# Issuing y's transfers in the block that computes y, and one product of four units a block later

## The chip, the core and the metric

The kernel runs on one core of one Trainium2 chip. The metric is device time in microseconds of one execution. The engines are TensorE (PE, with its weight loads PEld), VectorE (DVE), ScalarE (ACT), GpSimd (POOL) and SyncE (SP), whose queue issues nearly all DMA transfers. Each engine works through its own instructions in the order in which the program writes them, and waits at semaphores for the others. Lines are given as L1167, line 1167 of the kernel before.

## What is computed

The first part is a linear recurrence over 768 steps for 4 batches of 8 heads, with a 40 by 40 state each; the second is a feed-forward with a hardswish on the 3072 tokens of 320 features that come out of it.

```python
for t in range(S):
    y[:, :, t] = np.einsum('bhd,bhde->bhe', rt, state)
    Sa = np.einsum('bhde,bhe->bhd', state, at)
    state_decay = state * wt[:, :, None, :] - np.einsum('bhd,bhe->bhde', Sa, bt)
    state = state_decay + np.einsum('bhd,bhe->bhde', vt, kt)
...
h = x @ w_in
relu6 = np.clip(h + 3.0, 0.0, 6.0)
g = h * relu6 / 6.0
return (g @ w_out).astype(np.float32)
```

## The kernel before

**Units.** The recurrence is cut into 24 units, numbered 0 to 23: 64 steps of two batches with all heads. Four units form a group (`NU = 4`). Within a unit the steps are turned into matrix products: a first set, `prepare`, needs only the inputs and may run ahead (W and its running products `gam`, A, B, K, F, E, `factor`, EV); a second, `step`, needs the state left by the unit before (RT, VT, R, C, S, U, UT, rS, H, and `ysn`, which gives y and the new state). EV (L745) is scores times v: 32 small matmuls whose result `R` adds to much later. A triangular inverse of each group (`invert`, L779) runs on DVE in small steps between the other work.

**y to the feed-forward.** `ysn` (L1055) multiplies on PE (L1064), DVE adds (L1071), and POOL scales by `gam` into the tile `yg` (L1072). Then `move` issues four transfers from `yg` into `xt`, the layout that the feed-forward reads (L1111), and `move2` another four (L1116) and sets `ready[i]`. All eight are on SP's queue, between the fetches of inputs (`fetch`, L451; L478 for R and A, L490 for W, B and K, L487 for V) and the outputs (L1239). A fetch is written behind the instruction that has read the old contents of its tile, and waits for it.

**Order in blocks.** From unit 4 on, the program writes four blocks per unit, numbered here from 0 (`a_block`, L1505). Unit i's `ysn` stands in block 4(i-4)+4, its transfers in the next one. A unit's `prepare` begins at block `begins[i]`: units 8 to 11 at blocks 0, 3, 6 and 9, from 12 on every four blocks. Units 8 to 11 follow `CLOSE_STAGES`, the others `AHEAD_STAGES`; both lists give the stages for successive blocks. A block has two parts: the own unit's stages and the `prepare` of units that began at a multiple of four are in the first, the others in the second. `together` (L1468) writes a part: first the PE work of its stages in the order of `PRODUCTS`, then what DVE, ACT, POOL and SP do with the results in the order of `RESULTS`. Products of a part share pairs of PSUM banks, 512 columns each; two pairs take turns, and the next user of a pair waits until what was in it is read.

**The feed-forward between.** Behind each part, `feed` writes a few pieces of the feed-forward (`feed_forward`, L1140). Its jobs are half units (i, r), in a fixed list. A job has four expand pieces (L1167, x by `win`, into two PSUM tiles `h`), a short piece for the last 64 features (L1167 with 64 rows, or L1180 in a doubled 64-column form when no VT, B or factor stands beside it), ACT's and DVE's hardswish `gt` (L1189, L1190), and four contract pieces (L1215). The contract pieces of a job are written behind the expand pieces of the next one. If the next job's unit is not in `ready`, the contract pieces come at once and then nothing, until the unit is ready. The number of pieces per block is fixed by rates: 2.8 for units 4 to 6, then 3.5 or 4.5 times 8/9, and 6.2 where an inversion runs. A piece is 8 PE records (each float32 matmul leaves two), about 1 us.

After the last block the rest of the feed-forward is written without anything between.

Of the kernel before, what the change touches and what calls it, by code (L numbers as in the profile page):

```python
# [31 lines left out]
def kernel(  # L32
# [43 lines left out]
    B, H, T, D = r.shape  # L76
# [485 lines left out]
    def begun_beside():  # L562

        begin = -(-(SCAN + 1) // 16) * 16
        for n, name in enumerate("KB"):
            x = area[:, begin + n * H * JOIN:begin + (n + 1) * H * JOIN]
            nc.gpsimd.memset(x, 0.0)
            beside[name] = x.rearrange("p (h t) -> p h t", h=H)
        beside["E"] = grp.tile([P, H, BL], F32, name="E", tag="U", bufs=1)
        nc.gpsimd.memset(beside["E"][:], 0.0)  # L570
        for name in "rgam", "RT":
            beside[name] = tmp.tile([P, NPR, P], F32, name=name, tag="rgam", bufs=2)
# [191 lines left out]
    def in_turn(stages, order):  # L764

        for name in order:
            yield from stages[name]()
            shared[0] = None
            yield DONE
# [510 lines left out]
    third, F, group_F = [], None, []  # L1280
# [11 lines left out]
    def prepared(i):  # L1292
        nonlocal F
        if i >= NK:
            return None
        if i % NU == 0:
            F = lazy_F()
        return prepare(i, F)
# [145 lines left out]
    for _ in range(18):  # L1444
# [5 lines left out]


    EARLY_STAGES = [["fade"], ["RT", "VT"]]
    OWN_STAGES = EARLY_STAGES + [[], ["R", "C", "S"], ["U", "UT", "rS"], ["H"], ["ysn"],
                                 ["move", "move2"]]
    AHEAD_STAGES = [["W", "gam"], ["A", "B"], ["F", "K"], ["E", "factor"], ["EV"]]
    CLOSE_STAGES = [["W", "gam"], ["A", "B"], ["F", "K", "factor"], ["E"], ["EV"]]


    PRODUCTS = ["W", "S", "K", "VT", "B", "factor",
                "ysn", "EV", "R", "C", "U", "UT", "rS", "H", "E", "F"]  # L1460
    RESULTS = ["ysn", "W", "VT", "EV", "R", "S", "C", "A", "B", "move", "move2",
               "U", "UT", "rS", "F", "K", "fade", "H", "E", "factor", "RT", "gam"]
    TURNS = PRODUCTS[:3]
    WIDTH = {"R": NPR * D, "U": 512, "UT": 0, "ysn": NPR * JOIN, "EV": NPR * D}
# [3 lines left out]
    def together(stages):  # L1468
# [3 lines left out]
        def finish():  # L1472
            begun.sort(key=lambda x: RESULTS.index(x[0]))
            for _, rest in begun:
                for _ in rest:
                    pass
            begun.clear()
            shared[0] = open_half[0] = None
            ring.clear()
            ring.extend(TURNS_IN)  # L1480
# [24 lines left out]
    def a_block(m):  # L1505

        if coming and begins[coming[0]] == m:
            u = coming.popleft()
            close = coming and begins[coming[0]] < m + BLOCKS
            ahead[u, m] = prepared(u), CLOSE_STAGES if close else AHEAD_STAGES  # L1510
        i, early = (m + len(EARLY_STAGES)) // BLOCKS + NU, m + len(EARLY_STAGES)
        if m >= 0 and early % BLOCKS == 0 and i < NK:
            own[i, m] = step(i), OWN_STAGES
        parts = {}, {}
# [21 lines left out]
    begun_beside()  # L1536
    own[NU, -len(EARLY_STAGES)] = step(NU), OWN_STAGES
    for _ in in_turn(own[NU, -len(EARLY_STAGES)][0], [x for stages in EARLY_STAGES for x in stages]):
# [62 lines left out]
```

## Time and profile before

| | us |
|---|---|
| median of 3 runs (lowest to highest) | 781.25 (779.56 to 782.09) |
| profiled execution | 778.37 |
| its span, first to last instruction | 776.6 |
| PE busy | 714.2 |
| DVE busy | 508.0 |
| ACT busy | 310.1 |
| POOL busy | 176.4 |
| PE expand, L1167 | 228.9 |
| PE contract, L1215 | 230.4 |

The profiled execution is one execution of the program, recorded by the profiler; all positions below are microseconds from its first instruction. In a line of the timeline the first number is the start and the second the duration; in brackets is how long the engine stood idle before it and what ended the wait. The granted clock is the share of full speed at which the chip lets TensorE run; its mean over this execution is 0.964.

### The profile page before, as it was taken

To read this page: it belongs to the slowest core of one execution; us is meant where nothing else is said; L and a number is where in the kernel's file an instruction comes from. 1 tells how busy PE (TensorE), PEld (TensorE's weight loads), DVE (VectorE), ACT (ScalarE), POOL (GpSimd) and SP (SyncE) were. 2 spreads that over 40 slices of the span, in tenths; PEclk is the share of its full clock that TensorE was granted. 3 is DMA by queue.
4 is the path that set the end of the run, shared out by engine and by line. 5 is a ranking of instruction groups with operands and counts; after the bars stand their busy time and mean duration, and the time that the engine had idled before them with its cause. 6 is when DMAs were issued, how large, how long until landed. Compare 5 with 4: busy or idle time off the path is not lost.

```text
span 776.6 us, 33024 instructions
## 1 busy us (share of the span) xinstructions
PE 714.2 (92%) x14568; PEld 604.4 (78%) x14568; DVE 508.0 (65%) x1007; ACT 310.1 (40%) x644; POOL 176.4 (23%) x323
## 2 busy tenths in 40 slices
PE   5735888999899989999999999999999999999997
PEld 4634787878778778788888788888788888888885
DVE  7899967588657799456798356898446982323210
ACT  2377865323444334443334443234443224412211
POOL 7403110322233303123213122304122201110000
PEclk9956789999999999999999999999999999999999
DMA  9685553420434412233313223313232100110000
GB/s 124 122 189 133 113 169 60 78 40 19 78 62 85 74 43 53 43 66 67 59 43 57 55 62 67 59 44 61 52 62 53 29 19 24 35 35 12 13 18 19
DMA packets 176000, 48.44 MB, mean 62 GB/s; under 512 B 159216, under 2 KB 174576, under 8 KB 175856
## 3 DMA queue, kind: packets, MB, share of 16 engines
q1 hardware_dynamic: 171552, 45.58, 29.5%
q8 instruction: 115, 1.88, 1.0%
q10 hardware_dynamic: 4304, 0.74, 0.7%
q14 instruction: 29, 0.24, 0.1%
HBM read 37.62 MB, written 3.93 MB: 54 GB/s over the span
## 4 chain that ended last, share of the span: by engine, by line
PE 71%; DVE 13%; SPq 5%; issue 4%; ACT 3%; DMA 3%; POOL 0%; DVEq 0%; ACTq 0%; POOLq 0%
PE h L1167 24%; PE o L1215 22%; PE pair L554 4%; PE pair L1064 4%; DVE prod L804 2%; PE h L1180 2%; DVE x L810 2%; SPq L490 2%; PE one L506 2%; DVE prods L603 2%; PE pair L927 1%; PE pair L1007 1%; PE pair L516 1%; PE pair L968 1%; PE pair L1023 1%
## 5 line engine op out<-in xcount | busy, mean ns | idle before, releaser
L1167 PE MATMUL h<-xt,win 128*128 128x128 f32 (+1 forms) x2000 | 228.9, 282 | 8.4 <-DMA xt<-yg 4.2
L1167 PEld LDWEIGHTS h<-xt,win 128*128 128x128 f32 (+1 forms) x2000 | 211.9, 192 | 24.2 <-issue 7.7
L1215 PE MATMUL o<-wout,gt 128*128 128x320 f32 x768 | 230.4, 443 | 0.0
L1215 PEld LDWEIGHTS o<-wout,gt 128*128 128x128 f32 x768 | 138.7, 191 | 50.6 <-issue 0.6
L1189 ACT ACTIVATE gt<-h,three 128x512 f32<-128x512 f32 x96 | 62.5, 685 | 108.3 <-PE h L1167 86.0
L1190 DVE SCALAR_TENSOR_TENSOR gt<-gt,h 128x512 f32<-128x512 f32 x96 | 61.8, 680 | 63.8 <-ACT gt L1189 63.7
L578 DVE COPY_PREDICATED area<-mask,pair 128x512 f32<-128x512 int32 x56 | 40.7, 726 | 61.2 <-PE pair L554 42.7
L804 DVE TENSOR_TENSOR prod<-x 128x30 f32<-128x30 f32 (+9 forms) x180 | 63.8, 354 | 8.9 <-POOL x L789 2.5
L810 DVE TENSOR_TENSOR x<-x,prod 128x30 f32<-128x30 f32 (+9 forms) x180 | 63.3, 352 | 5.4
L1072 POOL TENSOR_TENSOR yg<-ys,gam 128x512 f32<-128x512 f32 x20 | 25.5, 1274 | 129.1 <-DVE ys L1071 87.5
L725 POOL TENSOR_TENSOR KBt<-K,rgt 128x320 f32<-128x320 f32 x22 | 19.0, 865 | 141.1 <-ACT rgt L714 118.7
L603 DVE TENSOR_TENSOR_SCAN prods<-area,start 128x528 f32<-128x528 f32 x24 | 40.9, 1708 | 3.8 <-ACT area L599 3.7
L1071 DVE TENSOR_TENSOR ys<-pair,ys 128x512 f32<-128x512 f32 x20 | 13.8, 690 | 41.3 <-PE pair L1064 41.3
L757 ACT ACTIVATE EV<-pair 64x320 f32<-64x320 f32 x44 | 19.0, 431 | 37.9 <-PE pair L752 37.5
L1064 PE MATMUL pair<-area,KBt 64*64 64x104 f32 x1280 | 32.4, 250 | 0.0
L1233 ACT ACTIVATE ob<-o 128x320 f32<-128x320 f32 x22 | 9.6, 435 | 56.7 <-PE o L1215 35.2
L614 DVE TENSOR_TENSOR_SCAN area<-area,start 128x528 f32<-128x528 f32 x24 | 31.2, 1301 | 0.8
L1064 PEld LDWEIGHTS pair<-area,KBt 64*64 64x64 f32 x1280 | 29.9, 133 | 1.5 <-issue 1.4
L872 ACT ACTIVATE tinv<-pair 32x256 f32<-32x256 f32 x48 | 18.0, 374 | 32.6 <-PE pair L862 32.1
L993 POOL COPY area<-V 128x320 f32<-128x320 f32 x20 | 9.0, 452 | 82.4 <-DVE area L645 51.3
L938 ACT ACTIVATE VT<-pair 128x512 f32<-128x512 f32 x22 | 13.1, 597 | 30.2 <-PE pair L705 16.2
L931 DVE TENSOR_TENSOR RR<-pair,EV 128x320 f32<-128x320 f32 x22 | 10.7, 486 | 20.8 <-PE pair L554 14.8
(289 smaller groups left out, 1093.4 us busy)
## 6 DMA issues: line engine op xcount, KB each, us to landing
V<-in_v_dram SPq DMA_DIRECT2D x96, 40.0 KB
out_dram<-ob SPq DMA_DIRECT2D x47, 80.0 KB
R<-in_r_dram SPq DMA_DIRECT2D x92, 40.0 KB
B<-in_b_dram SPq DMA_DIRECT2D x42, 80.0 KB
K<-in_k_dram SPq DMA_DIRECT2D x42, 80.0 KB
W<-in_w_dram SPq DMA_DIRECT2D x37, 80.0 KB
A<-in_a_dram SPq DMA_DIRECT2D x37, 80.0 KB
xt<-yg SPq DMA_DIRECT2D x72, 40.0 KB
```

The costliest lines, as they stand in the source:

```text
L554: nc.tensor.matmul(out=o[i][half(q), n ^ (2 * q * placed), :], lhsT=lhs[half(i, D), n ^ (2 * q * swap), half(q)], rhs=rhs[half(i, D), n, h ...
L578: nc.vector.copy_predicated(out=x[:].rearrange("p (i h) t -> p i h t", i=2), mask=mask8, data=o[2])
L603: nc.vector.tensor_tensor_scan(out=prods[:].rearrange("p r m i -> p (r m i)"), data0=wm[:, 0:SCAN], data1=start[:], initial=0.0, op0=ALU.m ...
L614: nc.vector.tensor_tensor_scan(out=back, data0=back, data1=start[:], initial=0.0, op0=ALU.mult, op1=ALU.add)
L804: nc.vector.tensor_tensor(out=pv, in0=_ap(x[:], (i + 1) * L + i, [[L, n], [0, i]]), in1=_ap(x[:], i * L, [[0, n], [1, i]]), op=ALU.mult,)
L810: nc.vector.tensor_tensor(out=rest, in0=rest, in1=pv, op=ALU.add)
L1064: nc.tensor.matmul(out=both[q][half(s), pr, :], lhsT=o[name][half(q), h * D:h * D + SLOT], rhs=beside[name][half(q), 4 * rs + 2 * (s ^ (q ...
L1072: nc.gpsimd.tensor_tensor(out=yg[:], in0=m["ys"][:].rearrange("p r q t -> p r (q t)"), in1=o["G"][:], op=ALU.mult)
L1167: nc.tensor.matmul(out=hp[c][:, i, :], lhsT=lhsT, rhs=rhs, start=(begun[c] == 0), stop=(begun[c] == 3 * NQ - 1))
L1189: nc.scalar.activation(out=gt[:], in_=hp[c][:], func=AF.Relu, bias=three[:], scale=1.0)
L1190: nc.vector.scalar_tensor_tensor(out=gt[:], in0=gt[:], scalar=6.0, in1=hp[c][:], op0=ALU.min, op1=ALU.mult)
L1215: nc.tensor.matmul(out=op[:], lhsT=gts[c][:, n, :], rhs=wout[:, c * HJ + r * NQ + n, :], start=((split or r == 0) and c == 0 and n == 0), ...
```

## The change

Three lists are edited. `ysn`, `move` and `move2` stand in one block, so that each unit's transfers are written in the block of its `ysn`. In `RESULTS` the two come directly behind `ysn` and `W`, ahead of all else in that part. In `CLOSE_STAGES` an empty block is put ahead of EV: for units 8 to 11 it goes from blocks 4, 7, 10 and 13 to 5, 8, 11 and 14.

```diff
-    OWN_STAGES = EARLY_STAGES + [[], ["R", "C", "S"], ["U", "UT", "rS"], ["H"], ["ysn"],
-                                 ["move", "move2"]]
+    OWN_STAGES = EARLY_STAGES + [[], ["R", "C", "S"], ["U", "UT", "rS"], ["H"],
+                                 ["ysn", "move", "move2"]]
     AHEAD_STAGES = [["W", "gam"], ["A", "B"], ["F", "K"], ["E", "factor"], ["EV"]]
-    CLOSE_STAGES = [["W", "gam"], ["A", "B"], ["F", "K", "factor"], ["E"], ["EV"]]
+    CLOSE_STAGES = [["W", "gam"], ["A", "B"], ["F", "K", "factor"], ["E"], [], ["EV"]]
...
-    RESULTS = ["ysn", "W", "VT", "EV", "R", "S", "C", "A", "B", "move", "move2",
+    RESULTS = ["ysn", "W", "move", "move2", "VT", "EV", "R", "S", "C", "A", "B",
                "U", "UT", "rS", "F", "K", "fade", "H", "E", "factor", "RT", "gam"]
```

`ready[i]` is set in `move2`, so it too is set a block earlier. No instruction is added or taken away.

## The prediction

> **What bounds the kernel now.** I read the page's busy shares first, then the waits of the TensorE queue (PE) from 200 us on, then the timelines around them. PE carries the span:
>
> ```profile
> PE 714.2 (92%) x14568; PEld 604.4 (78%) x14568; DVE 508.0 (65%) x1007; ACT 310.1 (40%) x644; POOL 176.4 (23%) x323
> ```
>
> Most of PE's idle time lies in the first 110 us, ahead of what the change touches. From 200 us on, PE's waits by engine and line are (total us, times, longest):
>
> ```profile
> PE h L1167 <- DMA xt<-yg: 4.2, 3, 1.8
> PE pair L752 <- DVE area L645: 1.9, 1, 1.9
> PE h L1167 <- DVE gt L1190: 1.4, 3, 0.7
> PE pair L1023 <- ACT UT L1013: 1.1, 1, 1.1
> PE pair L554 <- DVE E L578: 0.6, 1, 0.6
> ```
>
> So the rest of the kernel is PE's work plus about 9 us of waits, and PE executes in the order written. The change adds no instruction; it can only remove waits, make new ones, or reorder. I therefore count waits, against the profiled execution: 778.37 us, span 776.6. That run is 2.88 us under the median of 781.25 us; the result is put on the median.
>
> **What it removes.** First the three waits for y's transfers, 4.2 us. One of them:
>
> ```profile
> 316.04 3.12 SPq L1111 DMA_DIRECT2D xt<-yg  x4
> 320.45 3.55 PE L1167 MATMUL h<-xt,win 128*128 128x128 f32 x31 [1.66 <-DMA xt<-yg]
> ```
>
> Unit 7's y is ready at 306.67 (POOL's product at 305.40, 1.27 us), but its transfers stand behind A's in SP's queue and start at 316.04; matmuls start 1.29 us after the fourth issue ends (319.16). Issued in y's own block, behind W alone (307.23, 1.35 us), they start about 308.6 and are down 10 us before PE needs them. Units 11 and 15 are alike. **Gain 4.2.**
>
> Second, unit 11's EV (L752). The columns are start, duration, operation; then the granted clock in two stretches:
>
> ```profile
> 279.58 0.68 PE L752 MATMUL pair<-V,E 64*64 64x40 f32 x32 [1.91 <-DVE area L645]
> 280.18 2.02 PE L1167 MATMUL h<-xt,win 128*128 128x128 f32 x8
> 282.00 3.16 PE L1215 MATMUL o<-wout,gt 128*128 128x320 f32 x8
> ```
> ```profile
> 276.87:280.28 3.41, 1.50 (x41) 1.00 0.00 0
> 280.28:283.69 3.41, 3.41 (x12) 0.50 0.42 91
> ```
>
> PE stood 1.91 us behind DVE, which runs the inversion there. A block later DVE has passed that point: **gain 1.9**. The stretch after it ran at half clock: eight records took 1.82 us to the next start where 1.00 is usual (243.87 to 244.87), and the next eight 2.99 where 2.26 is usual (287.55 to 289.81). **Gain 1.6.** (The Trainium skill, "TensorE: Matmul & The Clock Gate", Part 1, has the clock halve after at least one idle window of about 3.4 us. Here 1.91 us of idle in one such window was enough, and 1.66 us ahead of 320.45 was not. By the page this 1.6 would not exist and the sum below would be +6.2; the row decides, so the page's result gets no chance of its own.)
>
> Third, waits for gt, 0.69, 0.33 and 0.34 us (270.89, 390.69, 503.73). They come where a job's last expand piece falls behind ysn; with pieces a little ahead it falls in front. I take the last two, **gain 0.7**; at the first, DVE is full and the next wait for it (E, 0.60 us at 274.99) takes it over. Fourth, the short piece: counting the order through all blocks, 25 instead of 19 are in the doubled 64-column form, 0.92 us (301.98 to 302.90) against 1.00 (272.38 to 273.38): **gain 0.5**. Sum of gains: 8.9.
>
> **What it adds.** The one place where the feed-forward's order changes is unit 4. In block 4 three pieces are issued behind ysn: two contract pieces of job (3,0), then a third. Now unit 4 is not yet ready, so the third is a contract piece of (3,1) and the stream runs dry until block 6. After the change `ready[4]` is set ahead of them, so the third is unit 4's first expand piece, and PE meets it before the data:
>
> ```profile
> 214.36 0.62 PE L752 MATMUL pair<-V,E 64*64 64x40 f32 x32
> 214.91 2.42 PE L1215 MATMUL o<-wout,gt 128*128 128x320 f32 x8
> 216.79 1.28 POOL L1072 TENSOR_TENSOR yg<-ys,gam 128x512 f32<-128x512 f32 x1 [0.89 <-DVE ys L1071]
> 218.34 1.34 PE L1215 MATMUL o<-wout,gt 128*128 128x320 f32 x4
> 219.59 3.14 SPq L1111 DMA_DIRECT2D xt<-yg  x4
> ```
>
> y is there at 216.79+1.28 = 218.07; four issues take 3.14, the landing 1.29: 222.50. PE arrives at 218.34 less 0.55 (unit 8's EV, gone from this block): 217.79. **Loss 4.7**, and as a whole window is idle, half clock behind it, **loss 1.6** by the row above. Nothing hides it: PE had no wait over 0.5 us between 205 and 270, and everything behind it in order shifts.
>
> Next, PSUM. Products of a part share pairs of banks, 512 columns each, and two pairs take turns. In block 8 factor and F of unit 10 (256+256) fill one pair. With EV of unit 9 in the same part it is factor+EV, and F takes the other; so unit 6's R in block 9 must wait for factor's copy, which ACT does behind F's six. In the trace F's multiply starts at 239.74 and the copy (L714) ends at 243.02, 3.28 later; where PE waits for such a copy it starts 0.38 after it (U at 226.91, copy's end 226.53). PE needs 0.6+1.0+0.5 = 2.1 from F to R, so the wait is 3.7-2.1 = 1.6, I take **loss 1.5** (bounds 0.5 and 1.8).
>
> Last, SP's queue, which from 229 to 266 us never rests, as units 9 to 11 come three blocks apart:
>
> ```profile
> 235.39 4.68 SPq L478 DMA_DIRECT2D R<-in_r_dram  x8
> 240.18 2.65 SPq L478 DMA_DIRECT2D A<-in_a_dram  x4
> 242.87 2.58 SPq L487 DMA_DIRECT2D V<-in_v_dram  x4
> 245.56 1.95 SPq L490 DMA_DIRECT2D B<-in_b_dram  x2
> 247.64 1.27 SPq L490 DMA_DIRECT2D K<-in_k_dram  x2
> 248.96 3.67 SPq L1111 DMA_DIRECT2D xt<-yg  x4
> ```
>
> Unit 5's eight transfers (248.96 to 255.13, 6.2 us) move ahead of V, B and K. B of unit 11 is landed at 249.42 by the packets' record, 1.9 after its last issue; PE uses it at 251.03: cover 1.6. I count both from unit 10's W on PE (228.62). R's fetch starts when RT is turned, 6.8 after it; with gt of job (4,0) now ahead on ACT and DVE, 7.5. From there to B's last issue 12.1 now, plus 6.2, plus 1.2 for unit 3's output, which falls in here: 19.5; landing 1.9: 28.9. PE comes 22.4 after W now; five contract pieces (1.2 each) for four expand and a short one (5.1 together) add 0.9, R's wait 1.5: 24.8. **Loss 4.1** (bounds 0 and 5), and half clock again, **loss 1.6** (or 0). The moves ahead of A in later blocks cost nothing: SP stands 43.8 us in 13 places ahead of A's fetch for DVE's turn of A (L528) as it is, and A is next used three or more blocks on.
>
> Losses 4.7+1.6+1.5+4.1+1.6 = 13.5; gains 8.9; net +4.6 us: 783.0 against the profiled execution's 778.4, **785.8 us** against the median, 0.6% slower.
>
> **Rivals.** (A) SP keeps up and B is in time. For it: the estimate subtracts two long chains. Against it: 6.2 us are put ahead of a cover of 1.6. Then 5.7 falls away: -1.1, 780.1. (B) Faster: PE's 4.7 us at unit 4 let ACT and SP catch up, so neither R nor B is late. It decides from the point where SP starts R under 2 us after W of unit 10 instead of 7.5. Then 7.2 falls away: -2.6, 778.6. Against it: R's fetch starts from DVE's transposes, which shift with PE. (C) DVE is busy without rest from 263 to 316 us, so PE, once EV no longer waits, meets DVE at the next product (F at 316.75 has 2.4 us of cover): the 3.5 is given back, +8.1, 789.4. Against it: one or two more pieces lie in front by then, 1 to 2 us. (D) The order at unit 4 stays as it is, so only the waits for y and EV go (-7.7) and R and B come (+7.2): 780.7. The job list speaks against it.
>
> **Numbers.** Forecast 0.47, A 0.18, B 0.15, C 0.17, D 0.03. The forecast's own range is 782.5 to 788, by the bounds of R, B and the clock; taking in A, C and D gives 779.5 to 790, with B left out. A measurement of this kernel can tell about 0.3% (2.3 us) from no change. Slower: forecast less its low edge, and C, 0.62; same: A, D and that edge less A's own low edge, 0.21; faster: B and A's low edge, 0.17.
>
> **What would show it.** A wait for xt of some 4.7 us ahead of the first expand of unit 4 near 218 us, with half clock behind it; no other wait for xt; no 1.9 us ahead of L752 near 280; a wait at L927 for rgt near block 9; a wait at L516 for B of unit 11. If PE's idle time from 200 us on falls from 9 us instead of rising to 12 or 13, the losses are wrong: most likely B, whose wait hangs on the order of SP's queue.

## The result and the profile after

The changed kernel takes 792.61 us (median of 4 runs, 788.94 to 793.93) beside 780.4 us for the kernel before (4 runs): a ratio of 1.0153, 95% interval 1.011 to 1.0196. Slower was forecast, at 785.8 us; the time lies 4.6 us over the top of the forecast's own range (782.5 to 788) and 2.6 us over the wider one that takes in its rivals (779.5 to 790). Its profiled execution took 791.58 us, with a span of 789.9. `ysn` of unit 4, the last work that the edit leaves alone, starts at 213.93 us (before: 212.88); from there to the end of the span it is 576.0 us (before: 563.7). So 12.3 us come from behind that point.

The page's busy shares of the kernel after; the columns are as before:

```profile
PE 722.3 (91%) x14664; PEld 611.4 (77%) x14664; DVE 510.7 (65%) x1007; ACT 310.6 (39%) x644; POOL 175.2 (22%) x323
```

PE is busy 8 us more with the same work (the 96 further records are six short pieces in the doubled form, which leaves 32 records for 16). PE's waits from 205 us on:

```profile
PE h L1167 <- DMA xt<-yg: 4.5, 1, 4.5
PE pair L516 <- DMA B<-in_b_dram: 3.3, 2, 2.9
PE pair L554 <- DVE E L578: 2.0, 1, 2.0
PE pair L1023 <- ACT UT L1013: 1.1, 1, 1.1
PE pair L927 <- ACT F L695: 1.1, 1, 1.1
```

The first, second and fifth are the three new waits that were forecast (4.7, 4.1 and 1.5). The three old waits for xt and that of EV are gone. The third row is longer than before (0.6): C of unit 7 behind E of unit 11. The fourth lies ahead of `ysn` of unit 4 and is the same in both kernels. All waits that the view lists behind that `ysn`, six small rows among them, are 13.1 us together, before 8.1.

Where the 8 us of busy time come from is seen in the granted clock. The columns are the stretch, its length, PE's busy time and records, the clock, and the DMA share and rate; each stretch is about 3.41 us, the step in which the clock changes:

```profile
215.64:219.05 3.41, 3.38 (x80) 1.00 0.38 66
219.05:222.47 3.42, 0.00 (x0) 1.00 0.12 40
222.47:225.88 3.41, 2.35 (x11) 0.50 0.09 22
225.88:229.29 3.41, 3.41 (x100) 0.50 0.50 99
229.29:232.71 3.42, 3.42 (x24) 0.50 0.18 30
232.71:236.12 3.41, 3.41 (x123) 1.00 0.02 5
```

Behind the wait at unit 4 the clock stays at half for three stretches, not one. After the waits for B and for C it is two each:

```profile
263.40:266.84 3.44, 0.58 (x3) 1.00 0.36 59
266.84:270.25 3.41, 2.95 (x12) 0.50 0.73 129
270.25:273.67 3.42, 3.42 (x21) 0.50 0.23 46
290.70:294.15 3.45, 1.77 (x56) 1.00 0.11 29
294.15:297.57 3.42, 3.11 (x41) 0.50 0.24 58
297.57:300.98 3.41, 3.41 (x13) 0.50 0.08 18
```

That is 23.9 us at half clock behind 205 us, where the kernel before had 3.4 (the last 0.8 and 1.4 us of the two spans left out). The profiled execution is no exception: the mean clock of the four executions is 0.945 to 0.955, its own 0.950; that of the kernel before lies between 0.951 and 0.971 in the 71 executions beside the experiments.

### The profile page after: what moved, and what is told of

Its sections match the earlier page's. It is cut to its first block, busy times and chain, and to the rows that moved or that the text cites. A ratio compares the mean times of both kernels' runs of the same rounds, so it can differ in the third digit from the quotient of the medians.

```text
span 789.9 us, 33195 instructions
## 1 busy us (share of the span) xinstructions
PE 722.3 (91%) x14664; PEld 611.4 (77%) x14664; DVE 510.7 (65%) x1007; ACT 310.6 (39%) x644; POOL 175.2 (22%) x323
## 4 chain that ended last, share of the span: by engine, by line
PE 63%; DVE 13%; SPq 7%; issue 6%; DMA 5%; ACT 3%; POOL 2%; POOLq 0%; DVEq 0%; ACTq 0%
PE h L1167 21%; PE o L1215 20%; PE pair L554 4%; DVE prod L804 3%; PE pair L1064 3%; DVE x L810 3%; SPq L490 3%; PE h L1180 3%; PE one L506 2%; PE pair L927 1%; DVE gt L1190 1%; PE pair L1007 1%; PE pair L516 1%; PE pair L1023 1%; DVE prods L603 1%
## 5 line engine op out<-in xcount | busy, mean ns | idle before, releaser
L1215 PE MATMUL o<-wout,gt 128*128 128x320 f32 x768 | 232.9, 448 | 0.0
L1167 PE MATMUL h<-xt,win 128*128 128x128 f32 (+1 forms) x1904 | 223.1, 284 | 7.2 <-DMA xt<-yg 4.5
L1167 PEld LDWEIGHTS h<-xt,win 128*128 128x128 f32 (+1 forms) x1904 | 208.2, 195 | 19.4 <-DMA xt<-yg 4.6
L1215 PEld LDWEIGHTS o<-wout,gt 128*128 128x128 f32 x768 | 140.3, 192 | 52.5 <-issue 1.8
L804 DVE TENSOR_TENSOR prod<-x 128x30 f32<-128x30 f32 (+9 forms) x180 | 65.6, 364 | 8.3 <-POOL x L789 2.7
L931 DVE TENSOR_TENSOR RR<-pair,EV 128x320 f32<-128x320 f32 x22 | 10.7, 485 | 35.8 <-PE pair L554 22.5
L1071 DVE TENSOR_TENSOR ys<-pair,ys 128x512 f32<-128x512 f32 x20 | 13.7, 684 | 23.7 <-PE pair L1064 23.6
L972 ACT ACTIVATE area<-pair 128x320 f32<-128x320 f32 x20 | 8.8, 438 | 50.9 <-PE pair L1007 43.3
L1180 PE MATMUL h<-xt,win 64*64 64x128 f32 x800 | 28.2, 275 | 0.0
```

Of the source, the lines that this page charges most:

```text
L804: nc.vector.tensor_tensor(out=pv, in0=_ap(x[:], (i + 1) * L + i, [[L, n], [0, i]]), in1=_ap(x[:], i * L, [[0, n], [1, i]]), op=ALU.mult,)
L1167: nc.tensor.matmul(out=hp[c][:, i, :], lhsT=lhsT, rhs=rhs, start=(begun[c] == 0), stop=(begun[c] == 3 * NQ - 1))
L1180: nc.tensor.matmul(out=hp[c][half(z), i, :], lhsT=y[:, half(z)], rhs=xt[half(c), 2, :], start=(begun[c] == 0), stop=(begun[c] == 3 * NQ - 1))
L1215: nc.tensor.matmul(out=op[:], lhsT=gts[c][:, n, :], rhs=wout[:, c * HJ + r * NQ + n, :], start=((split or r == 0) and c == 0 and n == 0), ...
```

## The experiments

All are compared with the kernel before on the same chip; ratios have their 95% intervals. How far two changed kernels lie apart is taken from their two ratios (0.1% is 0.8 us), since not all ran on one chip. The theory after the result: the forecast waits exist and are separate, and what was left out is the time at half clock behind each; the gain at EV of unit 11 is given back. The rivals: PSUM runs short through EV's move; or SP's queue is the whole loss.

**y's transfers alone** (EV where it was).

```diff
-    CLOSE_STAGES = [["W", "gam"], ["A", "B"], ["F", "K", "factor"], ["E"], [], ["EV"]]
+    CLOSE_STAGES = [["W", "gam"], ["A", "B"], ["F", "K", "factor"], ["E"], ["EV"]]
```

> y's transfers early, EV where it was. Theory (the loss is PE waiting for unit 4's y and then, behind SP's moved queue, for B of unit 11, each with half clock behind it): both waits stay, 4.5 and about 3 us, no wait at R of unit 6, the wait of EV of unit 11 may come back; no wait for xt but unit 4's. Time 9 to 13 us over the kernel before. Rival (the loss comes from EV sharing a part with factor and F, so that PSUM runs short): time within 3 us of the kernel before, or under it by the 4.2 us of waits for xt.

Measured 787.86 us, 1.0127 (1.0085 to 1.0169). The waits for xt at unit 4 (4.1) and for B (3.1) are there, none at R (L927), and 0.8 of EV's is back. The rival falls: with EV untouched most of the loss remains, 9.9 us by the ratio, at the low end of the 9 to 13 expected (by the medians it is 7.6). In its profile both waits have one stretch at half clock behind them; for unit 4:

```profile
220.90:224.31 3.41, 0.00 (x0) 1.00 0.12 38
224.31:227.72 3.41, 3.29 (x30) 0.50 0.24 52
227.72:231.13 3.41, 3.41 (x112) 1.00 0.39 73
```

The wait is nearly that of the changed kernel, but PE resumes at 224.43, at the start of a stretch, and fills it. In waits the two kernels are alike (13.7 us behind `ysn` of unit 4, and 13.1 in the changed one); what the changed kernel has more of is half clock.

**EV alone** (the same line of the kernel before edited, nothing else).

> EV of units 8 to 11 a block later, y's transfers where they were. Theory: a wait of about 1 us at R of unit 6, no 1.9 us wait at EV of unit 11 nor half clock behind it, the three waits for xt as before (4.2 us), no wait for B; time 0 to 4 us under the kernel before. Rival (PSUM runs short): 5 us or more over it.

Measured 782.79 us, 1.0037 (1.0011 to 1.0064): not under the kernel before, so the expectation missed, and the rival's 5 us are not there either. EV's wait is gone, R's is 0.2 us only, but waits for gt (1.8), xt (4.5 and 0.8) and the inversion's products come to the same. From `ysn` of unit 4 (215.39) to the end of the span it is 564.5 us against 563.7 before; the rest of its profile's difference lies ahead of unit 4, which the edit doesn't touch. So EV's move by itself gains nothing.

**The transfers early, but the feed-forward's order as before**: a unit is entered in `ready` a block later.

```diff
-                                 ["ysn", "move", "move2"]]
+                                 ["ysn", "move", "move2"], ["go"]]
...
+        def s_go():
+            ready[i] = m["xt"]
+            yield from ()
```

> As the changed kernel, but a unit counts as ready for the feed-forward only a block later, as before; the transfers stay early. Theory: the order of the feed-forward is that of the kernel before, so the wait of 4.5 us for unit 4's y and the 10 us of half clock behind it are gone; SP's order is that of the changed kernel, so PE still waits for B of unit 11 (1 to 5 us). Time 7 to 11 us under the changed kernel, within 5 us of the kernel before. Rival (SP's queue is the whole loss): within 3 us of the changed kernel.

Measured 785.59 us, 1.0063 (1.0037 to 1.009), 7.0 us under the changed kernel. No wait for xt is left, so the wait at unit 4 hangs on the order alone. SP's order by itself makes PE wait for B, longer than the 1 to 5 us expected: counted from `ysn` of unit 4, PE reaches B 10.7 us earlier than in the changed kernel (39.3 for 50.0), the last issue of B's fetch ends only 8.0 earlier (43.5 for 51.6):

```profile
PE pair L516 <- DMA B<-in_b_dram: 5.9, 2, 5.7
PE h L1172 <- DVE gt L1195: 3.2, 5, 1.1
```

**Early from unit 7 on, EV where it was.**

```diff
+    OWN_LATE = OWN_STAGES[:-1] + [["ysn"], ["move", "move2"]]
...
-            own[i, m] = step(i), OWN_STAGES
+            own[i, m] = step(i), OWN_LATE if i < 7 else OWN_STAGES
```

> y's transfers early from unit 7 on alone, late for units 4 to 6, EV where it was. Theory: every new wait of the changed kernel hangs on units 4 to 6 or on EV, and the three waits for xt (4.2 us) go: 3 to 5 us under the kernel before. Rival (early transfers cost SP's other fetches time everywhere): not under the kernel before.

Measured 774.5 us, 0.9933 (0.9907 to 0.9959): 5.2 us faster than the kernel before, a little more than expected. The three waits for xt are gone and nothing has come; early transfers do not cost SP's other fetches time in general.

**Unit 4 late, the others early**, with EV moved: `OWN_LATE if i in (4,)`.

> The changed kernel with unit 4's transfers (and its readiness) a block later, as before; all others early. Theory: the wait for xt at unit 4 (4.5 us) and the half clock behind it go; SP's order around unit 5 stays, so the wait for B of unit 11 stays or grows (3 to 6 us), with half clock. Time 5 to 9 us under the changed kernel. Rival (only SP's order around unit 5 matters): within 3 us of the changed kernel.

Measured 783.35 us, 1.0054 (1.0027 to 1.0081), 7.7 us under the changed kernel, as expected. The wait for B is 4.6 us. The rival falls.

**Unit 5 late, the others early**: `OWN_LATE if i in (5,)`.

> The changed kernel with unit 5's transfers a block later, as before; unit 4's and all others early. Theory: B, K and V of units 10 and 11 stand ahead of them again, so the wait for B (3.3 us) and its half clock go; the 4.5 us at unit 4 stay. Time 4 to 7 us under the changed kernel. Rival (the wait at unit 4 is the whole loss): within 3 us of the changed kernel, with a wait elsewhere.

Measured 784.4 us, 1.0067 (1.0041 to 1.0092), 6.7 us under the changed kernel, as expected. Its waits:

```profile
PE h L1167 <- DMA xt<-yg: 4.5, 1, 4.5
PE pair L554 <- DVE E L578: 2.0, 1, 2.0
PE pair L839 <- DVE state L1075: 1.9, 2, 1.3
PE pair L862 <- DVE area L645: 1.7, 2, 1.5
```

No wait for B at L516 is left. So that wait comes from unit 5's eight transfers standing ahead of B's fetch. In SP's queue of the changed kernel they do (start, duration):

```profile
245.97 4.49 SPq L478 DMA_DIRECT2D R<-in_r_dram  x8
250.56 1.86 SPq L478 DMA_DIRECT2D A<-in_a_dram  x4
252.52 1.68 SPq L1239 DMA_DIRECT2D out_dram<-ob  x2
254.30 3.08 SPq L1111 DMA_DIRECT2D xt<-yg  x4
257.43 2.47 SPq L1116 DMA_DIRECT2D xt<-yg  x4
259.94 2.99 SPq L487 DMA_DIRECT2D V<-in_v_dram  x4
263.06 2.43 SPq L490 DMA_DIRECT2D B<-in_b_dram  x2
```

SP does not rest from 245.97 on, and PE stands at L516 from 263.98 to 266.91 for this B.

**The wait at unit 4 filled with work.** 18 matmuls of the identity, whose result the first real matmul overwrites, stand ahead of unit 4's first expand matmul.

```diff
+        if xt is ready.get(NU) and j0 == 0:
+            for _ in range(18):
+                nc.tensor.matmul(out=hp[0][:, 0, :], lhsT=ident[:], rhs=ident[:], start=True, stop=True)
```

> The changed kernel with 18 matmuls of the identity ahead of unit 4's first expand matmul, whose result is overwritten: about 4.4 us of PE work where PE waits 4.5 us. Theory (the half clock behind a wait costs time of its own): the clock stays full behind it, the wait shrinks to under 1 us, and with the same data arriving at the same time the kernel is 2 to 5 us under the changed one. Rival (the half clock is only a record, PE loses nothing by it): within 1.5 us of the changed kernel, or over it.

Measured 784.93 us, 1.0057 (1.0026 to 1.0088), 7.5 us under the changed kernel, more than the 2 to 5 expected, with more work in it. Unit 4's first expand matmul starts at the same place, 9.60 us behind `ysn` of unit 4 in the changed kernel and 9.61 here. From there to F of unit 9 the same work takes 9.08 us in the changed kernel (223.53 to 232.61):

```profile
223.53 2.05 PE L1167 MATMUL h<-xt,win 128*128 128x128 f32 x8 [4.51 <-DMA xt<-yg]
225.37 1.06 PE L949 MATMUL one<-ident,state 128*128 128x128 f32 x4
232.61 0.71 PE L685 MATMUL pair<-bt,at 40*64 40x64 f32 x32
```

and 5.23 us here (225.07 to 230.30):

```profile
225.07 1.13 PE L1170 MATMUL h<-xt,win 128*128 128x128 f32 x8 [0.31 <-issue]
226.04 0.60 PE L949 MATMUL one<-ident,state 128*128 128x128 f32 x4
230.30 0.69 PE L685 MATMUL pair<-bt,at 40*64 40x64 f32 x32
```

So the three stretches cost 3.85 us. The rest of the 7.5 comes later: PE waits 1.8 us for B instead of 3.3, without half clock behind it, and behind C of unit 7 one stretch at half clock is left instead of two.

**The same filling with unit 5 late**, so that no wait for B can mix in.

> The kernel with unit 5's transfers late, and the 18 overwritten identity matmuls ahead of unit 4's first expand matmul. No wait for B is left in either, so the pair differs by the half clock behind unit 4's wait alone. Theory: no half clock there, 4 to 6 us under the kernel with unit 5 late. Rival (what filling won before was the wait for B, 1.5 us): within 2 us of it.

Measured 781.95 us, 1.0007 (0.9988 to 1.0027), against 1.0067 without the filling: 0.6%, 4.7 us. From unit 4's `ysn` to the end of the span it is 565.2 us against 570.1: 4.9. The waits of the two kernels are otherwise nearly the same, so this is the half clock behind one wait, almost by itself. Both figures lie over the rival's 2 us, though the two intervals taken at their near ends leave only 0.14% between the kernels.

**EV of unit 11 alone late, transfers early from unit 7 on.**

```diff
+ (CLOSE_STAGES[:-1] + [[], ["EV"]] if u == 11 else CLOSE_STAGES) if close else AHEAD_STAGES
```

> y's transfers early from unit 7 on, and EV a block later for unit 11 alone. Theory: the 1.9 us wait of EV of unit 11 and the half clock behind it go, nothing new comes: 2 to 4 us under the kernel with unit 7 on alone, 770 to 773 us. Rival (DVE is full there, so the wait comes back at the next product): within 1 us of that kernel, with a wait of 1.5 to 2 us for E's mask at C of unit 7.

Measured 775.84 us, 0.9954 (0.9937 to 0.9971), 1.6 us over the kernel without EV's move, with overlapping intervals. The theory falls. The rival is nearer, though neither its 1 us nor its place is met: EV's 1.9 us are gone and come back as waits for gt and for the inversion (L862, L839).

```profile
PE h L1167 <- DVE gt L1190: 2.8, 5, 0.9
PE pair L862 <- DVE area L645: 1.5, 2, 1.2
PE o L1215 <- issue: 1.4, 1, 1.4
PE pair L839 <- DVE state L1075: 0.8, 1, 0.8
PE pair L554 <- DVE E L578: 0.6, 1, 0.6
```

Without it, gt stood at 1.4 in three and neither L862 nor L839 showed a wait. For the 1.4 us put down to "issue" the profile shows no cause; waits of this kind of 0.9 to 1.4 us between 430 and 446 us appear in several of these kernels, at different lines, and not in others. What they are stays open.

**Units 4 and 5 late, EV moved.**

> The changed kernel with the transfers of units 4 and 5 a block later; the rest early, EV of units 8 to 11 late. Theory: the waits at unit 4 and for B are gone and only EV's move is left beside the gains: no wait over 1.2 us from 205 us on; small waits for gt, E and the inversion of 3 to 5 us together instead of EV's 1.9. Time 2 to 5 us under the kernel before, 0 to 3 us over the kernel with early transfers from unit 7 on alone. Rival (EV's move costs much by itself): not under the kernel before.

Measured 777.45 us, 0.9955 (0.9928 to 0.9982): no wait for xt or B, gt 3.2 us in five, as expected. What is left of EV's move wins nothing: beside the next kernel, which differs by EV's place alone, this one is 0.4% (3.1 us) slower, or 0.6 us by the profiles from `ysn` of unit 4 on.

**Early from unit 6 on, EV where it was.**

> y's transfers early from unit 6 on, late for 4 and 5, EV where it was. Theory: unit 6's transfers already stand clear of the full stretch of SP's queue, so the time is that of the kernel from unit 7 on (774 to 776 us), 3 to 6 us under the kernel before. Rival (SP is still full at unit 6): a wait for a fetch near 270 to 300 us, and 2 us or more over it.

Measured 774.54 us, 0.9915 (0.989 to 0.994), 6.6 us under the kernel before, the fastest of all by the ratio. Unit 6's transfers already stand clear; these are its first rows but for the wait that all kernels have ahead of unit 4:

```profile
PE pair L752 <- DVE area L645: 1.9, 1, 1.9
PE h L1167 <- DVE gt L1190: 1.4, 3, 0.7
PE pair L839 <- DVE state L1075: 0.8, 1, 0.8
```

EV of unit 11 waits 1.91 us here as in the kernel before, but the wait falls across two stretches, and the clock stays full:

```profile
275.92:279.33 3.41, 1.95 (x16) 1.00 0.24 58
279.33:282.75 3.42, 2.97 (x46) 1.00 0.27 58
```

The eight records behind it take 0.99 us to the next start (280.39 to 281.38) where the kernel before took 1.82.

No run separates the earlier block from the place directly behind `W` in `RESULTS`: all kernels with early transfers have both.

## Why the prediction was right in direction and too small

Point by point, against its own steps.

- **The three waits for xt, gain 4.2**: right. All three are gone in the changed kernel, and taking them alone (from unit 6 or 7 on) makes the kernel 0.7 to 0.9% faster, 5 to 7 us, somewhat more than their 4.2. With unit 6, 1.6 us of the rest is the half clock behind EV, which is not there in that profile; with unit 7 on, where it is there, the rest is open.
- **Unit 4, loss 4.7**: right, 4.5 measured. Late readiness or late transfers for unit 4 take it away; the order of the feed-forward is its cause, so rival D falls.
- **R of unit 6, loss 1.5**: 1.07. Counted from F, PE comes to it after 2.19 us (2.1 forecast), but R starts after 3.26 and not 3.7: it follows F's last copy on ACT (end 254.72) and starts at 254.77, before factor's copy ends (255.18). So it waits for F, not for factor as the prediction had it. It takes both parts of the change: with EV late and the old order at unit 4, another expand piece lies in front and the wait is 0.2.
- **B of unit 11, loss 4.1**: 3.3, and it goes with unit 5's transfers. Its two chains held almost to the term: from R's fetch to B's last issue 19.5 us (19.5 forecast), PE 24.9 behind W of unit 10 (24.8); only R's fetch starts 6.9 behind W and not 7.5. So rivals A (B in time) and B (R's fetch under 2 us behind W) fall.
- **"Half clock behind it, loss 1.6", twice**: the step that failed. The step took one stretch of 3.41 us behind each wait from the one row that the kernel before shows. There PE filled the stretch with 12 records of large matmuls. In the changed kernel the clock stayed at half for three stretches behind unit 4 (3.85 us lost, measured by the filling), two behind B and two behind C. Behind B, eight contract records took 4.56 us to the next start (268.25 to 272.81) instead of 2.26, and V's turn 0.62 instead of 0.39: with the rest 2.7 us. Behind C, 16 expand records took 3.57 (295.52 to 299.09) instead of 1.89, C itself 1.06 for 0.63, and the 1.9 us to the end of the stretch half again: 3.0 by estimate. Together 9.5 us, against 3.2 in the sum. The lines behind B and C:

```profile
268.25 4.63 PE L1215 MATMUL o<-wout,gt 128*128 128x320 f32 x8
272.81 0.69 PE L516 MATMUL pair<-ident,V 64*128 64x64 f32 x8
294.46 1.13 PE L554 MATMUL pair<-RT,VT 40*64 40x64 f32 x32 [1.99 <-DVE E L578]
295.52 3.78 PE L1167 MATMUL h<-xt,win 128*128 128x128 f32 x16
299.09 1.27 PE L1215 MATMUL o<-wout,gt 128*128 128x320 f32 x2
```

- **EV of unit 11, gain 1.9 and 1.6**: the second step that failed. Four pairs of kernels differ by EV's place alone: the kernel before and EV alone; from unit 7 on, without and with unit 11's EV late; from unit 6 on, and units 4 and 5 late; the transfers alone, and the changed kernel. In each the one with EV later is slower, by 0.2 to 0.4%, in three of them with overlapping intervals. So this part of the change is worth nothing or less. PE meets DVE elsewhere, near to what rival C had: where the order at unit 4 is the old one, at gt and the inversion; in the changed kernel at C of unit 7, 2.0 us with two stretches at half clock. That wait hangs on the order at unit 4 too: it is 1.6 with EV where it was and the transfers early, and 0.6 in every kernel with the old order at unit 4. Behind `ysn` of unit 4 PE's waits for DVE are 3.1 us, before 3.9: 0.8 won, where EV and gt were to bring 2.6.
- **gt, gain 0.7, and the short piece, 0.5**: the changed kernel's list has no row for gt, so all 1.4 us of it are gone there, but E's 0.6 has grown to 2.0; of the second, L1180 rose to 800 records for the 608 before, 25 pieces for 19, as counted; its time was not measured apart.

The terms with their measured sizes: waits +5.0 (13.1 less 8.1), half clock +7.9 (9.5 less 1.6), short pieces -0.5: 12.4, beside 12.3 in the profiles. The prediction had +3.5, +1.6 and -0.5, so its sum is 7.8 short. Of that, 3.3 is half clock behind the waits for unit 4's y and for B, 3.0 half clock behind C, 1.8 waits for DVE that did not go, 1.1 waits put down to issue and to the inversion's copy, less 1.4 by which the three forecast waits were too long. So the new waits and their places were right, the net term for the clock was a fifth of its size, and the one for EV should have been nothing. How many stretches follow a wait depends on where in a stretch PE resumes and on what it then runs (one behind 4.1 us, three behind 4.5), so a single row could not give that term; it needed a range of its own.

Ahead of 205 us the two kernels have the same order of work, and still their time at half clock differs there (51.2 us before, 54.6 after).

## What to carry to other kernels

When PE executes in order, moving a producer's transfers earlier is a gain only where the consumer's place in the order stays; if the same flag also moves the consumer, it lands in front of the data. Count every DMA issue that a moved step puts ahead of others on its queue, and compare it with the cover of each fetch behind it in the stretch where that queue never rests. And price a wait of PE not by its length alone: where it leaves enough of one stretch idle, it also costs the work done at half clock until PE has filled a whole stretch again. Work without use in such a gap can pay: here 18 overwritten matmuls in a wait of 4.5 us won 4.7 us.

## What the runs showed of the hardware

The clock fell to half after a stretch of 3.41 us with 1.50 us of busy time (41 records, mostly small; kernel before) and one with 1.77 (56 records, mostly small; kernel after, 290.70 us), and not after 1.75 (11 records, 317.83 us) or 1.73 (15 records, 546.49 us), large matmuls, in the kernel before, nor after 1.95 (16 records) and 2.97 (46), over which one wait of 1.91 us was split (from unit 6 on, 275.92 us). It came back after a stretch with 3.29 us busy (30 records) and after full ones with 7 to 36 records; it did not after 2.95, 3.11 and 3.15 us (12, 41 and 12 records), nor after full ones of 44 and of 100 records, mostly of small matmuls (the 44: transfers early and readiness late, 264.38 us). The Trainium skill, "TensorE: Matmul & The Clock Gate", Part 1, says that one busy window of about 3.4 us brings the full clock back, and that the windows run freely. The second agrees with the unlike lengths behind like waits (one stretch behind 4.1 us, three behind 4.5); the first does not hold here for every full stretch. The two that did not bring the clock back held 1.7 us or more of matmuls of 64 rows or fewer, those that did at most 1.1 us. That small matmuls count for less is read from these few rows and was not tried by itself.
